# A new hand-off order for one kernel's 660 operations, with D loaded first, added as column plus scalar, and the first copy on one engine

## The chip, the cores and the metric

The kernel runs on one core of one Trainium2 chip. The core has TensorE (PE, matrix products), VectorE (DVE), ScalarE (ACT), GpSimd (POOL) and SyncE (SP, which here only issues DMAs). The metric is device time in microseconds, the median of several runs.

## The reference

Two blocks, each behind a layer norm without weights, on a sequence of S = 2048 rows of D = 640 columns in bf16:

```python
# block A: a short filter over k, times v, then a long convolution along S
k_shift = sum over t<4 of k_pad[:, t:t+S] * shift_k[:, 3-t]
kv = k_shift * v
y = irfft(rfft(kv, 2S) * rfft(ssm_k, 2S))[:, :S] + kv * ssm_D
h = x + layernorm(x) * y            # x is A_q
# block B: dense, mish, dense
z = layernorm(h) @ w1 + b1          # 640 -> 1728
h2 = h + (z * tanh(softplus(z))) @ w2
```

The input B_x is not used.

## The kernel before

**How the work is staged.** The convolution is done as two-step Fourier transforms by matrix products, with the 640 columns in five blocks of 128 ("dc" 0 to 4). For the convolution kernel ssm_k: a block is loaded (`d_n0` to `d_n4`), ssm_D is added to its first column (`dadd0` to `dadd4`, L364; so kv * ssm_D needs no pass of its own), PE transposes it (`k1pe`, L370), a copy takes it from PSUM to SBUF (`k1ev`, through the helper at L254 to L258: L256 when ScalarE does it, L258 when VectorE does), PE does the first step of the transform in four quarters (`s1kpe{dc}_{quarter}`, L390 and L391, 16 matrix products each) and each is copied out (`s1kev`). When all twenty are there, the second step follows in 22 pieces over 128 frequencies (`s2kpe_{f}`, L416; `s2kev`), and ten DMAs make a copy with the halves swapped (`sw{dc}_{half}`, L444). For k and v: k is loaded in four parts (`d_k`), transposed (`ktpe{m}_{part}`, L335, five ops of 4 x 4 transposes), copied out (`ktev`), its last rows shifted by one on GpSimd (`ktsh`, L339), filtered by matrix products with a band matrix (`kspe{m}_{half}`, L351 and L352; the four band matrices `wsh0` to `wsh3`, L311, are built from `coef`, L303), and multiplied by v as it leaves PSUM (`kv{m}_{half}`, L356). It then goes through the same two steps (`s1vpe`, `s1vev`, `s2v{chunk}pe`, `s2v{chunk}ev`; the chunks are the dc blocks 0, then 1 and 2, then 3 and 4). The spectra are multiplied on VectorE (`pr{dc}_{f}`, L455, 20 of 128 x 2048), and two inverse steps bring them back: `i1pe`/`i1ev` (L473, twenty quarters) and `i2` (L525, by row tile), with `y{t}` as the copy out.

Sixteen row tiles t then follow: statistics of x (`ln1_t`, L504 and L505), 1/sqrt on GpSimd (`ln1p`, L509 to L511), the normalised x (`lnx`, L516 on ScalarE or L518 on GpSimd), the product with y (`wb`, L532), the sum with x (`h`, L534), the second norm (`bn`, L538 to L540; `pow`, L542; `hc`, L544), and a transposition (`trpe`/`trev` by PE for tiles 0 and 1; `tr` by DMA, L557, for the others). The dense layers go by units of tiles: units 0 and 1 have two tiles each, units 2, 3 and 4 have four. `m1pe{unit}_{pair}` (L582, L589) is the first product, `hb` (L604) mish on ScalarE, `m2pe{t}` (L647, L655) the second product, which is finished for two tiles at a time, `res{t}` (L672, L669) adds h on VectorE, and `d_out{t}` (L676) stores.

**What sets the order.** `ORDER` (L26 to L61) lists all 660 operations in the sequence in which they are issued. Each engine runs its own operations in that sequence, and waits for data where it must. `@0` to `@3` names which of four PSUM tiles (two banks each) an operation of PE writes; the tile can be written again when its copy out is done. `:a`, `:d` and `:p` put an operation on ScalarE, VectorE or GpSimd where it has a choice; without a letter the first in its list is taken. Loads are issued from SP in the order of the list, except `d_cst`, `d_dr` (D itself, 5 KB) and `d_sk`, which are issued from ScalarE's queue. Besides data and tiles, a DMA's issue waits for one of eight semaphores that the DMAs of these two queues use in turn.

In a list of operations below "PE, then ..." gives a sequence on one engine.

Of the kernel before, what the change touches and what calls it, by code (L numbers as in the profile page):

```python
# [30 lines left out]
s1kev2_1 ktpe1_3 ktpe4_0@2 wsh3 d_g0 ktev1 ktpe4_2 ktpe0_0@1 ktpe4_1 ktpe4_3 ktpe2_0@0 ktev4 ktpe3_0@3 ktpe2_2 ktpe3_3 d_g4 ktpe3_2 ktpe3_1 ktpe2_1
ktev3 s1kpe1_1@2 ktpe2_3 s1kev1_1 ktpe0_3 ktev2 ktpe0_1 ktsh3 d_g5 ktpe0_2 s1kpe3_0@3 ktsh1 s1kpe2_0@2 ktev0 ktsh4 s1kev3_0 kspe4_1@0 d_g3 ktsh2
s1kev2_0 ktsh0 kspe3_0@3 kv4_1 s1kpe2_3@1 s1kpe4_2@2 kv3_0 s1kev2_3 s1kpe4_0@0 s1kev4_2 s1kpe2_2@1 s1kev4_0:d kspe4_0@3 s1kev2_2 kspe0_0@2 kv4_0
s2kpe_96@0 s2kpe_30@1 kv0_0 s2kev_96 kspe1_0@3 s2kev_30 s2kpe_42@0 kv1_0 s2kpe_24@2 s2kev_42 kspe2_0@1 s2kev_24:d s2kpe_120@3 s2kpe_108@0 s2kev_120
kv2_0 kspe1_1@2 s2kev_108 s2kpe_12@3 kv1_1 d_x0 s2kpe_36@1 s2kev_12 d_x1 kspe0_1@0 s2kev_36:d s2kpe_90@2 s2kpe_48@3 s2kev_90 kv0_1 kspe2_1@1 s2kev_48
s2kpe_78@2 kv2_1 s1vpe4_1@0 s2kev_78 s2kpe_6@3 s1vev4_1 s2kpe_66@1 ln1_1 s2kpe_84@2 s2kev_66 kspe3_1@0 s2kev_84:d ln1p1 s2kev_6 s2kpe_0@1 kv3_1
s2kpe_60@2 s2kev_0 s1vpe2_0@3 s2kev_60 d_x2 s1vpe2_2@0 s1vev2_0:d s1vpe2_1@1 d_x3 s1vev2_2 s1vpe0_1@2 lnx1:p s1vev2_1:d s2kpe_102@3 s1vev0_1
s2kpe_72@0 s2kev_102:d s1vpe1_0@1 s2kev_72 s1vpe3_0@2 s1vev1_0 s1vpe0_2@3 s1vev3_0:d s1vpe1_3@0 s1vev0_2 s2kpe_126@1 ln1_0 s2kpe_114@2 s2kev_126
s1vpe2_3@3 s1vev1_3 s2kev_114:d s2kpe_54@1 ln1p0 s1vev2_3 s2kpe_18@0 s2kev_54:d s1vpe0_0@2 s2kev_18 s1vpe4_0@3 ln1_3 s1vpe3_2@1 s1vev0_0 sw2_1
s1vpe4_2@0 sw1_0 s1vev3_2:d s1vev4_0 ln1p3 s1vpe1_2@2 sw1_1 s1vev1_2 sw3_1 s1vpe1_1@3 s1vev4_2:d lnx3:p s1vpe3_3@1 sw4_1 s1vev1_1 s1vpe0_3@2  # L40
s1vev3_3:d lnx0:p sw3_0 s1vpe4_3@0 s1vev0_3 sw0_0 s1vpe3_1@3 ln1_2 sw2_0 s2v1pe_112@1 s1vev4_3 s2v1pe_96@2 sw0_1 s1vev3_1:d s2v1ev_112 ln1p2 sw4_0
s2v1pe_48@0 d_t2m s2v1ev_48 s2v1ev_96:d s2v1pe_32@1 lnx2:p s2v1pe_64@3 s2v1ev_32 s2v2pe_80@0 pr1_96 b1pe@2 s2v1ev_64 s2v1pe_80@1 pr1_32 s2v2ev_80
s2v1pe_0@3 s2v1ev_80:d s2v1ev_0 s2v1pe_16@0 s2v1ev_16 s2v2pe_32@3 pr1_64 s2v2pe_0@1 c_b1 s2v2ev_32 s2v2pe_48@0 pr1_0 s2v2pe_64@2 s2v2ev_48 pr2_64
i1pe1_0@3 s2v2ev_0 s2v2pe_112@0 pr2_96 s2v2ev_64 i1pe1_1@1 i1ev1_0 pr4_32 s2v2pe_16@2 s2v2ev_112 i1pe1_2@3 pr2_0 s2v2ev_16 pr2_32 s2v2pe_96@0 i1ev1_1
s2v0pe_0@2 pr3_0 i1ev1_2 i1pe2_3@1 s2v0ev_0 pr3_32 s2v0pe_64@3 s2v2ev_96 i1pe2_0@2 pr3_64 s2v0ev_64 s2v0pe_96@0 pr3_96 i1ev2_3 s2v0pe_32@3 pr4_0
i1ev2_0 i1pe2_1@1 d_w10 d_w11 s2v0ev_96 i1pe3_1@2 pr4_64 d_w12 i1ev2_1 d_w14 i1pe3_2@0 pr0_0 d_w13 s2v0ev_32 i1pe3_3@1 pr4_96 i1ev3_2 i1pe3_0@3
i1ev3_3 pr0_32 i1pe4_2@0 i1ev3_0 i1pe4_1@1 pr0_96 i1ev3_1 i1pe1_3@3 ln1_6 i1ev4_2 i1pe4_3@2 pr0_64 ln1p6 i1ev1_3 i1pe2_2@0 i1ev4_1 ln1_5 i1pe0_0@3
lnx6:p i1ev2_2 i1pe0_2@1 ln1_9 ln1p5 i1ev0_0 i1pe0_1@0 ln1_4 lnx5:p i1ev0_2 i1pe0_3@3 i1ev0_1:d ln1p4 i1ev4_3 i1pe4_0@1 ln1_7 i1ev0_3 ln1p9 d_w2b
i1ev4_0 d_w2c ln1_11 i2a1@0 d_w2a ln1p7 i2a0@2 i2b0 ln1_14 i2b1 i2pe9@3 y0 i2pe4@1 y1 wb0 i2a3@2 y9 h0 i2pe11@0 wb1 y4 i2b3 h1 i2a2@3 y11 bn0 i2b2
i2pe10@1 y2 i2pe5@0 y10 bn1 i2pe7@3 pow0 y3 i2pe6@1 y7 i2pe12@2 wb3 pow1 y6 hc0 h3 trpe0@3 y12 i2pe13@1 hc1 trev0:a wb2 trpe1@2 bn3 trev1:a i2pe8@3  # L50
y13 m1pe0_4@2 h2 pow3 y8 bn2 lnx9 ln1p11 m1pe0_2@1 hc3 y5 m1pe0_6@3 wb6 tr3 pow2 hb0_2 wb5 m1pe0_1@0 w2z lnx7 hc2 ln1_10 tr2 m1pe0_3@1 hb0_4 lnx11:p
hb0_6 h5 m1pe0_0@2 ln1p14 lnx4 ln1_15 hb0_3 m1pe0_5@3 h6 hb0_0 bn6 m1pe1_5@1 hb0_1 wb7 lnx14 pow6 m1pe1_4@2 bn5 ln1p15 hb1_5 m1pe1_1@0 hb1_4 hc6 h7
tr6 pow5 hb0_5 m1pe1_2@1 bn7 ln1p10 hb1_1 m1pe1_0@2 hc5 ln1_12 pow7 tr5 m1pe1_6@3 hb1_0 hc7 ln1p12 hb1_2 ln1_8 tr7 m1pe1_3@0 hb1_6 wb11 i2pe14@2 h11
hb1_3 wb4 i2pe15@1 wb9 lnx10 m2pe0@3 h4 h9 y14 bn4 lnx12 ln1_13 pow4 ln1p8 hc4 m2pe2@0 wb10 tr4 h10 ln1p13 lnx8 bn11 lnx15 bn10 pow11 y15 lnx13 wb8
pow10 hc11 m1pe2_3@2 res2 wb12 d_out2 h12 tr11 h8 m1pe2_2@1 wb14 res0 bn8 d_out0 m2pe1@0 bn9 pow8 wb13 pow9 hc8 hc10 wb15 tr10 h13 h14 m1pe2_4@3 hb2_3
hc9 tr8 bn13 hb2_2 tr9 h15 pow13 m1pe2_5@2 bn12 bn14 pow12 m1pe2_6@1 hb2_5 hc13 bn15 tr13 hb2_4 m2pe3@2 hc12 pow15 hb2_6 tr12 pow14 hc15 hc14 tr14
tr15 m1pe3_1@3 res3 res1 d_out3 d_out1 m1pe3_6@1 hb3_1 m1pe3_0@2 hb3_6 m1pe3_2@0 hb3_0 m1pe3_4@3 hb3_2 m1pe2_1@1 hb3_4 m1pe3_5@2 hb2_1 m1pe2_0@0 hb3_5
m1pe3_3@3 hb2_0 m2pe4@1 hb3_3 m2pe6@2 m2pe5@0 res6 res4 d_out6 d_out4 m2pe7@3 m1pe4_3@2 res7 res5 d_out5 d_out7 m1pe4_5@1 hb4_3 m1pe4_2@3 hb4_5
# [108 lines left out]
def kernel(  # L167
# [193 lines left out]

    k1_pes, k1_evs = [], []
    for b in range(NDC):
        dad = OP(f"dadd{b}", ["dve", "pool"], [d_n[b], o_dc], emit=lambda e, b=b: (nc.gpsimd if e == "pool" else nc.vector).tensor_tensor(raw_n[b][:, 0:1], raw_n[b][:, 0:1], dcol[:, b:b + 1], ALU.add))  # L364
        p_ = pt()

        def pe(e, b=b, p_=p_):
            o = p_.b16().rearrange("p (t d) -> p t d", t=NT)
            for t2 in [*range(1, NT), 0]:
                nc.tensor.transpose(o[:, t2, :], raw_n[b][:, t2:S:16], ident)  # L370
# [347 lines left out]
```

## Time and profile before

| what | us |
|---|---|
| median of 3 runs (228.49 to 228.54) | 228.52 |
| the profiled execution | 227.92 |
| its span, first to last instruction | 226.13 |
| outside the span | 1.79 |
| first second-step copy of ssm_k (`s2kev_96`) starts on ScalarE | 32.86 |
| last copy of the first inverse step (`i1ev4_0`) starts on ScalarE | 92.46 |
| first matrix product of the dense layers (`m1pe0_4`) | 102.07 |
| last piece of the residual sum (`res15b`) starts | 223.16 |

The span has three parts. Up to about 33 us the inputs come in and PE, VectorE and ScalarE hand small pieces to each other. From there to about 102 us the convolution runs, in which VectorE and ScalarE have hardly a pause. From 102 us to the end PE has no pause in the dense layers. Times of single operations come from the timeline of each engine, matched to `ORDER` by counting instructions.

### The profile page before, as it was taken

Reading aid. Unit: us, or ns where it says so; the run is one execution under the profiler, and the core shown is the slowest. Engines: PE = TensorE matmul, PEld = TensorE weight load, DVE = VectorE, ACT = ScalarE, POOL = GpSimd, SP = SyncE. Lnnn points to the kernel's source line nnn. Section 1 sums busy time; section 2 is a strip of 40 time slices with the busy share of each in tenths; the row PEclk is TensorE's granted clock in tenths of the full one; section 3 lists DMA queues with packets and bytes.
Section 4 is the critical chain, followed back from the end, with each engine's and each line's share of the span. In section 5 each row is a group of like instructions: output and inputs, shape, how many; then the busy total and the mean of one; then the engine's idle time right before and its main releaser. Section 6 shows DMA issues by size and latency. Waiting matters only on the chain.

```text
...
## 1 busy us (share of the span) xinstructions
...
## 2 busy tenths in 40 slices
...
GB/s 206 371 421 415 418 343 33 210 232 97 414 412 206 167 259 4 185 192 33 29 77 38 62 58 89 137 12 3 0 0 58 29 32 0 3 29 46 58 53 48
DMA packets 19563, 30.98 MB, mean 137 GB/s; under 512 B 10704, under 2 KB 14928, under 8 KB 18768
## 3 DMA queue, kind: packets, MB, share of 16 engines
...
q8 instruction: 21, 0.34, 0.6%
...
q0 software_dynamic: 96, 0.00, 0.0%
HBM read 20.42 MB, written 2.62 MB: 102 GB/s over the span
## 4 chain that ended last, share of the span: by engine, by line
PE 67%; DMA 9%; DVE 9%; ACT 7%; SPq 3%; issue 3%; POOL 1%; DVEq 0%; ACTq 0%
PE ps L647 25%; PE ps L582 25%; DMA ks<-in_A_ssm_k_dram 6%; DVE ks L455 5%; PE ps L473 3%; ACT uv L256 3%; ACT ks L256 3%; SPq L444 3%; DMA ks<-ks 3%; PE ps L335 2%; PE ps L416 2%; PE ps L351 2%; PE ps L390 2%; PE ps L352 1%; PE ps L589 1%
## 5 line engine op out<-in xcount | busy, mean ns | idle before, releaser
L604 ACT ACTIVATE ks<-ps,b1s 128x512 bf16<-128x512 f32 (+1 forms) x69 | 36.2, 617 | 44.0 <-PE ps L582 35.8
L647 PE MATMUL ps<-ks 128*128 128x320 bf16 (+2 forms) x420 | 58.6, 299 | 0.0
L582 PE MATMUL ps<-G 128*128 128x512 bf16 (+1 forms) x325 | 57.6, 337 | 0.1
L672 DVE TENSOR_TENSOR rb<-ps,rb 128x640 bf16<-128x640 f32 x15 | 11.8, 820 | 68.4 <-PE ps L655 66.0
L647 PEld LDWEIGHTS <-ks 128*128 128x128 bf16 x420 | 40.6, 98 | 17.3 <-issue 1.3
L582 PEld LDWEIGHTS <-G 128*128 128x128 bf16 x325 | 31.3, 98 | 24.7 <-issue 1.6
L256 ACT CAST uv<-ps 128x1024 bf16<-128x1024 f32 x50 | 46.6, 1145 | 0.0
L256 ACT CAST ks<-ps 128x640 bf16<-128x640 f32 (+3 forms) x46 | 37.9, 898 | 10.1 <-PE ps L391 6.7
L455 DVE TENSOR_TENSOR ks<-ks,uv 128x2048 bf16<-128x2048 bf16 x20 | 23.0, 1221 | 0.8 <-DMA ks<-ks 0.6
L416 PEld LDWEIGHTS <-G 128*128 128x128 bf16 x512 | 20.9, 96 | 3.1 <-issue 2.5
L473 PE MATMUL ps<-a_t,ks 128*128 128x128 bf16 x320 | 19.2, 219 | 1.3 <-DVE ks L455 1.2
L473 PEld LDWEIGHTS <-ks 128*128 128x128 bf16 x320 | 18.2, 113 | 1.8 <-DVE ks L455 1.6
L509 POOL TENSOR_SCALAR ve<-mv 128x1 f32<-128x1 f32 x16 | 4.7, 294 | 48.2 <-DVE mv L505 47.3
L542 POOL TENSOR_TENSOR r<-ve,mhalf 128x1 f32<-128x1 f32 x16 | 10.2, 638 | 21.7 <-DVE ve L540 21.7
L416 PE MATMUL ps<-uv,G 128*128 128x64 bf16 (+1 forms) x384 | 12.9, 187 | 1.7 <-ACT uv L256 1.4
L538 DVE BATCH_NORM_STATS2 st<-rb 128x6 f32<-128x320 bf16 x32 | 14.1, 482 | 0.1
L258 DVE CAST ks<-ps 128x1024 bf16<-128x1024 f32 (+1 forms) x12 | 14.0, 1179 | 0.2
L504 DVE BATCH_NORM_STATS2 st<-rb 128x6 f32<-128x320 bf16 x32 | 13.9, 475 | 0.0
L356 DVE TENSOR_TENSOR ra<-ps,rb 128x1024 bf16<-128x1024 f32 x10 | 11.9, 1219 | 1.1 <-PE ps L352 0.7
L258 DVE CAST uv<-ps 128x1024 bf16<-128x1024 f32 x10 | 11.9, 1211 | 0.5 <-PE ps L391 0.2
L390 PE MATMUL ps<-cst,ks 128*64 128x128 bf16 x160 | 10.8, 220 | 0.9 <-DVE ks L258 0.5
L390 PE MATMUL ps<-cst,ra 128*64 128x128 bf16 x160 | 10.5, 219 | 0.8 <-ACT uv L256 0.5
...
## 6 DMA issues: line engine op xcount, KB each, us to landing
...
```

What stands on the lines that cost most here:

```text
L256: nc.scalar.copy(o, i)
L258: nc.vector.tensor_copy(o, i)
L356: nc.vector.tensor_tensor(kv_w[:, m, :, 8 * h:8 * h + 8, :], p_.f32().rearrange("p (l t d) -> p d t l", l=4, t=8), raw_v[:, 8 * h:8 * h + ...
L390: nc.tensor.matmul(ps[0:64, dgl, :], lhs, mc, start=True, stop=True)
L416: nc.tensor.matmul(p_.f32()[:, o:o + n], g_v[:, f, :], src[:, :, f, :], start=True, stop=True)
L455: nc.vector.tensor_tensor(o, o, v, ALU.mult)
L473: nc.tensor.matmul(pz[:, dgl, :], KS[:, k, b, :, l], a12[:, k, :], start=k == 0, stop=k == 1)
L504: nc.vector.bn_stats(st1[:, t, hh, :], xt(t)[:, hh * 320:(hh + 1) * 320])
L538: nc.vector.bn_stats(st2[:, t, hh, :], xt(t)[:, hh * 320:(hh + 1) * 320])
L582: nc.tensor.matmul(ph[:, o:o + w], w1[:, dc, fc * P:fc * P + P], lt[:, dc, 0:w], start=dc == 0, stop=dc == NDC - 1)
L604: nc.scalar.activation(hb[:, fc, 0:n], p_.f32()[:, i * 512:i * 512 + n], ACT.Mish, bias=b1s[:, fc:fc + 1], scale=1.0)
L647: nc.tensor.matmul(p_.f32()[:, o:o + n], lhs, w2[:, k, cols:cols + n], start=fc == 0, stop=single and fc == 13)
```

## The change

The chunks and all sizes stay. Three small edits:

```diff
-dad = OP(f"dadd{b}", ..., (gpsimd or vector).tensor_tensor(raw_n[b][:, 0:1], raw_n[b][:, 0:1], dcol[:, b:b + 1], ALU.add))
+dad = OP(f"dadd{b}", ..., (gpsimd or vector).tensor_scalar(raw_n[b][:, 0:1], raw_n[b][:, 0:1], dcol[:, b:b + 1], None, ALU.add))
...
-k1_evs[b].append(OP(f"k1ev{b}" + "b" * h, ["act", "dve"] if h else ["dve", "act"], ...
+k1_evs[b].append(OP(f"k1ev{b}" + "b" * h, ["dve"] if b in K1S else ["dve", "act"], ...
```

The first makes the addition of D a column plus a per-partition scalar. The second takes away the choice for the two half copies of block 0: both are VectorE's (`k1ev0` was ScalarE's). The third is a new `ORDER`, all of it. Its beginning, and the stretches that are spoken of later:

```diff
-d_cst wz idn d_n0 cz d_dr wm@0 small lane d_n1 d_sk d_n3 warm d_n4 d_k2 kz d_a12 dsel dcol d_k0 dadd0:p k1pe0@1 d_n2 dadd1 d_k3 k1pe1@2 k1ev0b:d
-k1ev0:a d_k1 s1kpe0_3@3 k1ev1 s1kpe0_0@0 s1kev0_3 dadd3:p d_v2 s1kpe0_2@1 s1kev0_0:d s1kpe0_1@2 k1pe3@3 s1kev0_1 dadd4:p d_v3 s1kev0_2:d cfpe@0
...
+d_dr wz idn d_n0 cz wm@0 small lane d_n1 d_cst d_sk d_n3 warm d_n4 d_a12 kz d_n2 dsel dcol dadd0 k1pe0@1 d_k1 dadd1:p d_k3 k1pe1@2 d_k0 k1ev0b d_v3
+k1ev0 s1kpe0_2@3 k1ev1 s1kpe0_1@0 s1kev0_2 d_k2 s1kpe0_0@1 dadd3 s1kev0_0 s1kpe1_0@2 s1kev0_1:d d_v2 s1kpe1_3@3 s1kev1_0 d_v0 cfpe@1 k1pe3@0 coef
...
+s1kev3_3 ktsh0 s1kev2_2:d s1kpe1_2@0 s1kpe1_1@2 s1kev1_2 kv2_0 s1kpe2_3@3 s1kev1_1 s1kpe2_0@0 s1kev2_3:d kspe2_1@1 s1kev2_0 kspe3_0@2 kv2_1
+s2kpe_102@3 s2kpe_120@0 kv3_0 s2kev_102 kspe4_0@1 s2kev_120 s2kpe_18@3 kv4_0 s2kpe_114@2 s2kev_18 kspe0_0@0 s2kev_114 s2kpe_108@1 kv0_0 kspe1_0@3
...
```

What moves, engine by engine:

- **SP's queue** before: n0 n1 n3 n4 k2 a12 k0 n2 k3 k1 v2 v3 g1 v0 v1 and seven more g; after: n0 n1 n3 n4 a12 n2 k1 k3 k0 v3 k2 v2 v0 g3 g6 v1 and six more g. `d_x3` goes behind the ten `sw`, `d_t2m` behind four of the five `d_w1`. The two queues of DMAs together are the same set.
- **Copies**: `ktev0` and `ktev3` (128 x 2048) go from VectorE to ScalarE, `s2v1ev_80` and `s2v1ev_96` too; some thirty others change engine, so that ScalarE has 17 of the 22 `s2kev` instead of 16 and 12 of the 20 `s1vev` instead of 13.
- **GpSimd**: `wsh2` goes to VectorE; `dadd1`, `dadd2` and `dadd4` are GpSimd's (they were `dadd0`, `dadd3` and `dadd4`); `lnx` of tiles 4, 7, 8, 9, 10, 12 and 15 goes from ScalarE to GpSimd, which then has 14 of the 16. Tiles 8, 5 and 4 are normalised among the products `pr3`, and 10, 9, 12 and 15 follow in a row behind `pow6` and `pow4` (`pow6 pow4 lnx10 lnx9 lnx12 pow7 lnx15 pow11 pow5`).
- **The dense layers** before: units 0 and 1, `i2pe14`, `i2pe15`, then `m2pe0 m2pe2 m1pe2_3 m1pe2_2 m2pe1 m1pe2_4 ...`; after: units 0 and 1, the same two, then `m2pe1@2 m2pe3@1 m2pe0@3 m1pe2_3@0 m1pe2_0@1 m1pe2_6@0 m2pe2@2 m1pe3_0@1 m1pe3_1@2 m1pe2_5@3 ...`. VectorE's list beside it: `... wb5 hc6 h8 h11 hc4 bn7 h5 bn11 bn5 wb10 hc7 hc11 wb13 wb9 hc5 wb12 wb15 wb14 bn8 h13 res3 h14 h10 hc8 h15 h9 bn9 bn10 bn13 hc10 hc9 res1 bn14 bn15 hc13 h12 hc14 bn12 res2 ...`.
- **The end** before: `m2pe11 m2pe13 res11 res9 m2pe15b res13 res15b`; after: `m2pe12 m2pe14 m2pe15b res12 res14 res15b`, with the stores `d_out12 d_out14 d_out15b` last.

More of the change, by code (lines that the diff above doesn't have):

```diff
@@ L31 @@
[L31 to L58, printed above, removed]
@@ new lines @@
+s1kev1_3 dadd2:p d_g3 dadd4:p k1pe2@2 wsh3 k1ev3:a k1pe4@1 d_g6 k1ev2 s1kpe0_3@3 k1ev4 wsh1 s1kpe3_2@0 d_v1 s1kev0_3 s1kpe3_0@2 s1kpe4_3@1 s1kev3_2
+s1kev3_0:d s1kpe2_1@3 d_g7 s1kev4_3 wsh0 s1kpe4_0@0 s1kev2_1:d s1kpe3_1@2 s1kev4_0 ktpe3_0@1 d_g1 ktpe3_3 s1kev3_1:d s1kpe4_2@3 ktpe0_0@0 s1kev4_2
+ktpe3_1 wsh2:d ktpe1_0@2 d_g2 ktpe3_2 ktpe0_1 ktev3:a ktpe1_2 ktpe0_2 ktpe1_3 ktpe1_1 ktpe2_0@3 ktev1 ktpe2_2 d_g4 ktpe0_3 ktpe4_0@1 ktev0:a ktpe2_3
+ktsh1 ktpe4_3 ktpe2_1 d_g0 ktsh3 s1kpe4_1@2 ktev2 ktpe4_1 ktpe4_2 s1kev4_1 kspe1_1@0 ktev4 ktsh2 s1kpe2_2@3 d_g5 kv1_1 s1kpe3_3@2 ktsh4 kspe2_0@1
@@ new lines @@
+s1vpe3_0@2 s1vev3_3 sw3_1 s2v1pe_112@1 lnx3:p sw0_0 ln1_0 s1vev3_0 s1vpe0_3@3 sw4_0 s2v1pe_16@0 s2v1ev_112 pr2_64 sw3_0 ln1p0 s2v1pe_48@2 d_x3
+s2v1ev_16 s2v1pe_32@1 s1vev0_3:d lnx0:p s2v1ev_32 s1vpe3_1@0 pr1_64 s1vpe0_0@3 s2v1ev_48 s2v1pe_0@1 s1vev0_0:d s1vev3_1 s2v1ev_0 pr2_32 s2v2pe_32@2
+s2v2pe_112@0 s2v2ev_32 s1vpe0_1@3 pr2_0 s2v2ev_112 s2v2pe_48@1 s2v2pe_64@2 pr1_32 s1vev0_1 s2v2pe_0@0 pr2_96 s2v2ev_64 s2v0pe_32@3 s2v2ev_0
+s2v2pe_80@2 pr1_0 s2v2ev_48 i1pe2_0@0 pr1_96 s2v0ev_32 s2v2pe_16@1 ln1_8 s2v2ev_80 s2v0pe_0@3 pr3_32 s2v2ev_16 ln1p8 i1pe1_0@2 s2v0ev_0 ln1_5 lnx8:p
@@ new lines @@
+i1pe1_3@1 i1ev1_0 pr3_64 ln1p5 s2v2pe_96@3 i1ev2_0 s2v0pe_96@2 ln1_4 lnx5:p s2v2ev_96 s2v0pe_64@0 pr3_0 s2v0ev_96 ln1p4 i1pe1_2@3 d_w13 i1ev1_3 d_w12
+pr3_96 i1pe2_1@2 lnx4:p d_w14 i1ev1_2 d_w11 i1pe2_2@1 pr0_32 d_t2m s2v0ev_64 d_w10 i1pe2_3@3 pr0_0 i1ev2_1 i1pe3_3@0 i1ev2_2 pr0_96 i1pe3_0@2 i1ev2_3
+i1pe3_2@1 pr0_64 i1ev3_0 i1pe3_1@3 pr4_96 i1ev3_2 i1pe1_1@2 pr4_32 i1ev3_3 i1pe0_2@1 i1ev1_1 pr4_0 i1pe0_0@0 i1ev0_2 i1pe0_3@2 pr4_64 i1ev0_0
+i1pe0_1@1 ln1_7 i1ev3_1 i1pe4_3@0 ln1_6 i1ev0_3 ln1p7 i1pe4_2@3 i1ev4_3 ln1_11 i1pe4_1@2 ln1p6 i1ev0_1 i1pe4_0@0 i1ev4_2:d lnx7:p i1ev4_1 i2a0@1 d_w2b
@@ new lines @@
+ln1_13 i2a1@3 lnx6:p i1ev4_0 d_w2c b1pe@2 d_w2a ln1_15 ln1p11 c_b1 i2b0 i2a3@0 y0 i2b1 i2a2@2 y1 wb0 i2b3 i2pe13@1 h0 y3 i2pe12@3 wb1 y13 bn0 i2b2
+i2pe10@0 y2 i2pe11@1 y12 h1 i2pe4@2 pow0 y11 bn1 i2pe7@3 y4 i2pe8@1 y7 wb3 i2pe6@2 pow1 hc0 y8 h3 trpe0@3 y6 i2pe9@1 hc1 wb2 trev0:a trpe1@2 h2
+lnx11:p trev1:a i2pe5@3 bn2 y9 w2z m1pe0_5@2 y10 bn3 pow2 y5 m1pe0_2@1 hb0_5 hc2 pow3 wb4 m1pe0_6@0 tr2 hb0_2 ln1p13 m1pe0_4@3 hc3 wb6 tr3 wb8
+m1pe0_1@2 ln1p15 hb0_4 ln1_9 hb0_6 m1pe0_0@1 hb0_1 h6 ln1p9 ln1_12 lnx13 m1pe0_3@3 hb0_0 wb7 ln1p12 m1pe1_0@0 ln1_10 hb0_3 m1pe1_4@2 h7 hb1_0 ln1p10
```

22 lines of the change are left out of this document (16 added, 6 removed).

## The prediction

> **What bounds the kernel now.** I read the busy time of each engine in stretches first, cut where the timelines of ScalarE and PE change character.
>
> ```profile
> core 0: us, PE busy (x) PEld busy (x) DVE busy (x) ACT busy (x) POOL busy (x), PEclk, DMA share, GB/s
> 0.00:32.86 32.86, 29.89 (x564) 25.12 (x565) 24.45 (x31) 18.03 (x19) 14.47 (x28) 1.00 0.95 371
> 32.86:93.37 60.51, 56.08 (x1245) 52.51 (x1243) 58.47 (x72) 59.28 (x67) 13.49 (x28) 1.00 0.55 194
> 93.37:102.07 8.70, 8.24 (x65) 4.72 (x63) 8.39 (x25) 8.28 (x15) 3.80 (x8) 1.00 0.65 233
> 102.07:223.10 121.03, 121.03 (x821) 75.14 (x820) 48.93 (x124) 45.85 (x83) 20.62 (x38) 1.00 0.16 40
> 223.10:226.13 3.03, 0.03 (x1) 0.00 (x0) 0.42 (x1) 0.00 (x0) 0.00 (x0) 1.00 0.22 76
> ```
>
> From 102.07 PE is busy in every microsecond, at full clock: 121.03 us of dense products that the change does not touch. So a gain can only come from starting them earlier, and a loss also from holes in them. From 32.86 to 93.37 ScalarE and VectorE are both full (59.28 and 58.47 of 60.51 us). Before that neither is. The timelines of the first 17 us show where the hand-offs stall:
>
> ```profile
> 6.82 0.16 DVE L364 TENSOR_TENSOR ks<-ks,dcol 128x1 bf16<-128x1 bf16 x1 [0.80 <-DMA ks<-in_A_ssm_k_dram]
> 6.89 0.68 DVE L258 COPY ks<-ps 128x1024 bf16<-128x1024 bf16 x1
> 7.61 1.01 ACT L256 COPY ks<-ps 128x1024 bf16<-128x1024 bf16 x1 [3.63 <-DVE ks L258]
> ...
> 12.71 8.14 POOL L311 TENSOR_TENSOR rw<-cst,coef 128x1120 bf16<-128x1120 bf16 x4 [2.77 <-DVE coef L303]
> 15.30 1.52 DVE L364 TENSOR_TENSOR ks<-ks,dcol 128x1 bf16<-128x1 bf16 x1
> 16.87 0.28 PE L370 MATMUL ps<-ident,ks 128*128 128x128 bf16 x1 [0.41 <-DVE ks L364]
> ```
>
> The two halves of block 0's copy ran one behind the other although on two engines, the first behind `dadd1`. `dadd2`, one column, took 1.52 us instead of 0.16: it ended at 16.82, when GpSimd's second `wsh` did (16.80), and PE's last transposition of block 2 waited for it.
>
> **The first 33 us.** I laid out the new order by hand. An operation starts when its engine is free, its input is there and its PSUM tile was copied out, with start-to-start times from the timelines: a block of 16 transpositions 1.15 us, an `s1kpe` 0.45, a `ktpe` 0.25, a `kspe` 0.83; a copy of 1024 takes 0.91 on ScalarE (1.01 until its data can be used) and 1.13 on VectorE (1.22), one of 2048 1.86 and 1.13.
> - *D first.* D landed at 5.54, issued at 1.11; issued at 0.72 it lands 0.4 earlier. That is worth nothing: `dadd0` ended at 6.29, and PE's last transposition of block 0 began at 6.40, at its own pace.
> - *The addition.* On GpSimd a column of such a form costs 0.22 to 0.29 (L509) for 0.19: nothing, since PE reads that column last, 1 us behind the first. `dadd2` now stands ahead of the `wsh`: 1.4 us of VectorE and 0.4 of PE go.
> - *Both halves on VectorE.* 6.69 to 7.36 and 7.30 to 7.98 (0.68 each), for 7.58 and 8.62. PE is with block 1 until 7.92, so `s1kpe0` starts no earlier, but its second half at 8.37, not 8.68, and ScalarE is spared 1.01.
> - *Block 2's load* goes ahead of two 640 KB parts of k, 1.55 us each by the landings: 15.28 becomes about 12.2. All that is then late is k part 2, at 19.9 for 18.3 or so, and one `ktpe` waits some 0.4 us.
> - *The end of this stage* goes: `ktev0` on ScalarE ends 24.2, `kspe1_1` 25.2, `kv1_1` on VectorE 25.8 to 27.0 (behind `ktev4`), `s1kpe1_2` in its tile 27.7, `s1kev1_2` 27.75 to 28.75, `s1kpe2_0` 29.45, `s1kev2_0` 29.55 to 30.55, PE in `kspe3_0` until 31.0, `s2kpe_102` to 31.6, and its copy starts at 31.6.
>
> A layout by hand has no small gaps; I take **31.8** for 32.86. Ends: 31.1 if k's part 2 and block 2 land in time, 32.5 if each of some ten hand-offs loses 0.1 more.
>
> **From there to the last copy of the inverse step (ScalarE).** Before: start 32.86, last copy ends its share at 93.37: 60.5 us, of which 58.5 by counts (15 `s2kev` at 0.855 and a short one 0.31, 13 `s1vev`, 18 `s2v` copies and 19 `i1ev` at 0.905 to 0.91) and 2.0 are gaps (0.71, 0.70 and five small ones). After: one `s2kev` more, one `s1vev` fewer, two `s2v` copies more: +0.86 - 0.91 + 1.82 = +1.8, so 60.3. In the layout the two gaps of 0.7 shrink to 0.5 together, the small ones stay: 1.2 in all. 31.8 + 60.3 + 1.2 = **93.3**. What ScalarE was given is thus as much as the early start brings. VectorE loses two `s2v` copies and an `s2kev`, gains an `s1vev` and a statistic: -2 x 1.15 - 1.07 + 1.15 + 1.03 = -1.2, and would be free for `wb0` at about 92.3, where y0 ends at 94.0: no bound, with 1.5 us in hand. The swaps are issued about 52.6 (54.23 before) and the first two land 4.9 later, 57.5, just as VectorE comes to `pr2_64` (57.7). `d_t2m` behind four weight loads: issued about 80, landed by 89 at the 8.7 us of its row, wanted at 92. `wsh2` on VectorE, not shown before: between 0.65 (half of L455's 2048) and 2.06 us (its row on GpSimd); I take 1.3, the middle; VectorE waits there for k's part 2 anyway, from 19.1 to 21.6, so even 2.06 is hidden.
>
> **To the first dense product.** The same chain of y0, y1, `wb`, `h`, `bn`, `pow`, `hc`, `trpe`, `trev`: 8.70 us, so 102.0 for 102.07.
>
> **The dense layers.** PE's 121.03 us stay if it never waits. The narrow place is new: `m2pe2` wants tile 2 of PSUM, which `res1` frees. On PE: 16.2 us (units 0 and 1, two `i2pe`), three `m2pe` (10.97), two `m1pe2` at 2.215 and one at 1.78: 33.4 us after the first product. On VectorE: its list down to `res1` by start-to-start times (`wb` and `h` 0.40, `hc` 0.36, statistics 1.04, `bn` 1.22, `res` 0.73) ends 31.9 after the first product, if GpSimd never holds it up. Before, `res2` was ready 2.7 us before `m2pe1` wanted it. GpSimd does hold it up:
>
> ```profile
> 105.72 1.38 POOL L489 MEMSET ks<- 64x640 bf16 x2
> 107.10 0.86 POOL L518 TENSOR_SCALAR ra<-rb,r,nmr 128x640 bf16<-128x640 bf16 x1
> ```
>
> ```profile
> 105.70 0.83 DVE L544 TENSOR_SCALAR rw<-rb,mv,r 128x640 bf16<-128x640 bf16 x1 [0.44 <-POOL r L542]
> 107.48 0.82 DVE L534 TENSOR_TENSOR rb<-ks,rb 128x640 bf16<-128x640 bf16 x1
> 109.25 0.44 DVE L534 TENSOR_TENSOR rb<-ks,rb 128x640 bf16<-128x640 bf16 x1
> ```
>
> A sum that takes 0.44 took 0.82 and ended 0.34 after GpSimd's normalisation did; that is 0.4 us a time, and 0.8 in that stretch with one normalisation and the clearing. Now five normalisations are there: 0.8 + 4 x 0.35 = 2.2 if each hits such an operation, 0.8 if none does. About half do: 1.5, so `res1` ends at 33.4, when PE wants it. I take **0.3** us of holes (0 to 0.7).
>
> The Trainium skill, "SBUF — State Buffer", section "Who interferes with whom", says that a VectorE instruction with two SBUF inputs and a GpSimd instruction that reads SBUF exclude each other for the whole instruction. The trace agrees: `dadd2` ended with the `wsh`, the sum at 107.48 went on when the normalisation had ended. By that rule alone each of the four added normalisations may cost up to its 0.87: 0.8 + 3.5 - 1.5 = 2.8 us of holes, and about 231.3.
>
> **The end.** `res12` and `res14` (0.73 apart) fit under `m2pe15b`'s 1.5 us, but `d_out14` is issued just ahead of `d_out15b`, and of two stores in a row the second landed 0.5 later (181.92 behind 181.42): +0.1, at most 0.5.
>
> **The sum.** Span 226.13 - 0.07 (start) + 0.3 + 0.1 = 226.46, +0.33 on the profiled execution of 227.92. That run lies 0.60 under the median of the runs; on the median it is 228.52 + 0.33, **228.8 us**. A change under 0.2% (0.46 us) is about what a measurement of this kernel cannot tell from none.
>
> **The rivals.**
> - *The lead is kept (faster).* ScalarE starts at 31.3, its gaps are 0.6, PE has no hole: 31.3 + 60.3 + 0.6 = 92.2, -1.2, end +0.1: 227.4 (226.9 to 228.0). For it: 1.4 us of stall at `dadd2` really goes. Against: ScalarE is full, and gets 1.8 more.
> - *GpSimd holds VectorE (slower).* Past 1.5 us of hold-up between `hc1` and `res1`, each further one is a hole on PE in front of `m2pe2`, and 8, 5 and 4 among the products cost VectorE its 1.5 us before `wb0` likewise. With 2.2 to 2.5 in each: holes 0.7 to 1, first product 0.5 later: 229.9 (229.0 to 231.3). Against: VectorE's statistics, half its time there, were not held up in the rows.
> - *The early lead is not there (slower).* ScalarE starts at 32.2 with gaps of 1.6, so that its 1.8 more are not paid: 94.1, +0.7, holes and end +0.4: 229.6 (229.0 to 230.4). For it: the layout has nothing spare in it.
> - *The small edits do nothing by themselves:* D's early landing is idle here, as worked out; inside the forecast.
>
> **Chances.** Forecast, within 0.2%: 0.32, with a range of its own of 228.1 to 229.0. Kept lead 0.28. GpSimd 0.22, no lead 0.18: slower 0.40. Range for 8 in 10, cutting a tenth off the outermost cases on each side: 227.1 to 230.7.
>
> **What would show it.** `dadd2` on GpSimd at 0.2 to 0.3 us and no wait of PE for it; the first `s2k` copy on ScalarE at 31.1 to 32.5; ScalarE without gaps from there to about 93.3; `wb0` waiting for y0, not for VectorE; first dense product near 102.0; PE busy 121.0 us from there, or a hole before `m2pe2` with VectorE's `res1` as releaser; VectorE's `wb`, `h` and `hc` at 0.8 beside GpSimd's `lnx`. I am wrong if the first `s2k` copy is off by over 0.7 us, or if ScalarE waits in the product stage for `pr` results.

## The result and the profile after

The changed kernel is a little faster, by 0.2 to 0.4% in three comparisons, of which the last does not exclude no change. In the first comparison it takes 227.65 us (median of 19 runs, 227.05 to 228.72) where the kernel before takes 228.53 (19 runs), a ratio of 0.9959 [0.9945, 0.9973]. Run again unchanged on other chips it stood at 0.9982 [0.9966, 0.9997] and 0.9984 [0.9964, 1.0003], while the kernel before, run against itself, gave 1.0002 [0.9989, 1.0016] and 1.0002 [0.9982, 1.0022]. The forecast was no change, 228.8 us.

A trap stands at the start: the two profiled executions say the opposite of the medians. The changed kernel's took 228.13 us and the kernel before's 227.92. What the profiled times hang on is shown below; why the medians differ is not shown in full. The stretches of the changed kernel, cut at the same events as those shown of before (first copy `s2kev` on ScalarE, end of the last inverse copy's share, first dense product, last residual piece):

```profile
core 0: us, PE busy (x) PEld busy (x) DVE busy (x) ACT busy (x) POOL busy (x), PEclk, DMA share, GB/s
0.00:32.71 32.71, 30.20 (x564) 25.50 (x565) 22.65 (x31) 20.30 (x20) 12.77 (x27) 1.00 0.94 366
32.71:93.69 60.98, 56.97 (x1246) 53.41 (x1244) 57.88 (x73) 60.91 (x68) 27.80 (x36) 1.00 0.60 213
93.69:102.29 8.60, 7.96 (x63) 4.70 (x63) 8.26 (x24) 8.26 (x16) 3.90 (x7) 1.00 0.29 106
102.29:223.34 121.05, 120.73 (x815) 75.21 (x820) 47.56 (x122) 40.76 (x76) 22.06 (x39) 1.00 0.14 39
223.34:226.36 3.02, 0.01 (x1) 0.00 (x0) 0.42 (x1) 0.00 (x0) 0.00 (x0) 1.00 0.37 130
```

The first stretch is 0.15 us shorter, the second 0.47 longer, the third 0.10 shorter, the dense layers the same to 0.02. (Their row shows 0.32 us less of PE and six products fewer. The stretch is no longer for it, and the same kernel's second profile has all 821 products in the same time, so I take these for records that the trace lost.) ScalarE's idle time in the second stretch went from 1.23 us (60.51 less 59.28) to 0.07: it has more copies and no pauses. The timelines show where the pauses were. Before, and then after:

```profile
32.86 2.68 ACT L256 CAST ks<-ps 128x960 bf16<-128x960 f32 x3 [1.03 <-DVE ra L356]
36.13 2.68 ACT L256 CAST ks<-ps 128x960 bf16<-128x960 f32 x3 [0.59 <-PE ps L416]
39.40 2.68 ACT L256 CAST ks<-ps 128x960 bf16<-128x960 f32 x3 [0.59 <-PE ps L416]
```

```profile
32.71 8.02 ACT L256 CAST ks<-ps 128x960 bf16<-128x960 f32 x9 [1.03 <-DVE ra L356]
```

Nine copies stand in one row with no wait ahead of the later ones. And the two small stalls of the first stage are gone. GpSimd's two additions in the changed kernel, ahead of its `wsh`, and the two halves of block 0's copy on VectorE:

```profile
11.77 0.53 POOL L364 TENSOR_SCALAR ks<-ks,dcol 128x1 bf16<-128x1 bf16 x2 [3.88 <-DMA ks<-in_A_ssm_k_dram]
12.63 6.11 POOL L311 TENSOR_TENSOR rw<-cst,coef 128x1120 bf16<-128x1120 bf16 x3 [0.33 <-PE ps L370]
```

```profile
6.89 1.29 DVE L258 COPY ks<-ps 128x1024 bf16<-128x1024 bf16 x2 [1.39 <-PE ps L370]
```

In their place PE waits for a DMA, on the line that transposes k (L335). PE's waits in the first 33 us of the changed kernel (total, times, longest):

```profile
PE ps L286 <- DVE rw L281: 1.2, 1, 1.2
PE ps L370 <- DMA ks<-in_A_ssm_k_dram: 0.6, 1, 0.6
PE ps L335 <- DMA ra<-in_A_k_dram: 0.3, 1, 0.3
```

The 0.6 us on L370 (0.2 before) is the wait for block 1. The last row, 0.3 us, is the one that sets the time of the changed kernel's profiles, as the third group of experiments shows.

### The profile page after: what moved, and what is told of

Same layout as the page of the kernel before. It is cut to its first block, busy times and chain, and to the rows that moved or that the text cites. A ratio compares the mean times of both kernels' runs of the same rounds, so it can differ in the third digit from the quotient of the medians.

```text
span 226.4 us, 6193 instructions
## 1 busy us (share of the span) xinstructions
PE 215.9 (95%) x2684; PEld 158.8 (70%) x2690; DVE 136.8 (60%) x248; ACT 130.2 (58%) x177; POOL 66.5 (29%) x107
## 4 chain that ended last, share of the span: by engine, by line
PE 63%; DVE 16%; DMA 11%; ACT 6%; SPq 2%; issue 1%; ACTq 0%; DVEq 0%
PE ps L647 25%; PE ps L582 25%; DVE ks L455 10%; DMA ra<-in_A_k_dram 5%; ACT ks L256 3%; DMA ks<-in_A_ssm_k_dram 3%; DMA ks<-ks 2%; ACT uv L256 2%; PE ps L335 2%; DVE st L504 2%; PE ps L351 2%; SPq L444 1%; PE ps L416 1%; PE ps L473 1%; PE ps L390 1%
## 5 line engine op out<-in xcount | busy, mean ns | idle before, releaser
L256 ACT CAST uv<-ps 128x1024 bf16<-128x1024 f32 x51 | 47.3, 1173 | 0.0
L256 ACT CAST ks<-ps 128x960 bf16<-128x960 f32 (+3 forms) x47 | 38.1, 907 | 9.4 <-PE ps L391 8.1
L455 DVE TENSOR_TENSOR ks<-ks,uv 128x2048 bf16<-128x2048 bf16 x20 | 23.6, 1239 | 1.4 <-DMA ks<-ks 1.4
L518 POOL TENSOR_SCALAR ra<-rb,r,nmr 128x640 bf16<-128x640 bf16 x14 | 15.9, 1141 | 2.7 <-DVE ks L532 1.3
L509 POOL TENSOR_SCALAR ve<-mv 128x1 f32<-128x1 f32 x16 | 6.2, 388 | 35.3 <-DVE mv L505 34.4
L542 POOL TENSOR_TENSOR r<-ve,mhalf 128x1 f32<-128x1 f32 x16 | 10.1, 636 | 17.3 <-DVE ve L540 17.2
L416 PE MATMUL ps<-uv,G 128*128 128x64 bf16 (+1 forms) x384 | 13.4, 187 | 1.8 <-ACT uv L256 1.8
L510 POOL TENSOR_TENSOR r<-ve,mhalf 128x1 f32<-128x1 f32 x16 | 13.1, 819 | 1.3
L258 DVE CAST ks<-ps 128x1024 bf16<-128x1024 f32 (+1 forms) x11 | 12.9, 1187 | 0.4 <-PE ps L416 0.3
```

Source lines behind the costliest of these rows:

```text
L256: nc.scalar.copy(o, i)
L416: nc.tensor.matmul(p_.f32()[:, o:o + n], g_v[:, f, :], src[:, :, f, :], start=True, stop=True)
L455: nc.vector.tensor_tensor(o, o, v, ALU.mult)
L510: nc.gpsimd.tensor_tensor(r1[:, t:t + 1], ve1[:, t:t + 1], mhalf[:], ALU.pow)
L518: nc.gpsimd.tensor_scalar(lnx_s[t % 9], xt(t), r1[:, t:t + 1], nmr1[:, t:t + 1], ALU.mult, ALU.add)
```

## The experiments

Times are medians; each ratio is to the kernel before on the same chip. "Base B" is the kernel before, "base A" the changed one. Two distances recur: from PE's start on block 1 (`k1pe1`, which as a rule starts 0.05 us behind the landing of block 1) to ScalarE's first `s2kev`, and from there to the first dense product. The "front" is the part up to that `s2kev`, the "back" what follows.

**Which half holds the gain.** The changed order up to its first `s2kpe`, then the old one, and the reverse; the filter pieces that one half had already done were exchanged for those that it had not.

```diff
 fa_bb: ... kspe3_0@2 kv2_1          (changed order)
+       s2kpe_96 ...                 (order before, to the end)
 fb_ba: the order before up to s2kpe_96
+       s2kpe_102 s2kpe_120 ...      (changed order, to the end)
```

> The changed kernel once more, for a second profile. Theory F (the gain is made in the first 33 us, and the first profile caught a late execution): ratio to before 0.994 to 0.998, and a profile whose first second-step copy of ssm_k starts earlier than the 32.71 us of the first profile, at 31.5 to 32.3, with the first dense product at 101 to 102. Theory B (the gain is made after 33 us): the same ratio, but first copy again at 32.5 to 33 and the way from it to the first dense product 0.5 to 1 us shorter than the 69.2 us of before.

> The kernel before once more, against itself: ratio 0.998 to 1.002. Its profile is to show how far two executions of one kernel lie apart. Theory F: first second-step copy at 32.9 or later (the first profile, 32.86, was an early one, its execution 0.6 us under the median). Theory B: 32.7 to 33, and the way from there to the first dense product longer than 69.2 us.

> The changed kernel's first 33 us (its list up to kv2_1, with the two small edits), then the list of before from its first second-step piece on, with kspe and kv renamed so that each block half is still filtered once. Theory F: 0.5 to 1.5 us faster than before (0.993 to 0.998). Theory B: within 0.3 us of before, or slower.

> The first 33 us of before, then the changed kernel's list from its first second-step piece on, renamed likewise. Theory F: no gain, 0 to 1.5 us slower than before, since ScalarE has 1.8 us more copies and no earlier start to pay them from. Theory B: 0.5 to 1 us faster than before.

Unchanged kernels: 0.9982 and 1.0002; a_again's first `s2kev`, 31.98 us, is what theory F expected, b_again's, 32.40, is not. Hybrids: 229.42 (1.0056 [1.0043, 1.0068]) and 229.68 (1.0069 [1.0056, 1.0082]), both slower than either parent, by 1.3 us and more. Theory F fails in the first hybrid, theory B in the second. That an order fits the state in which the stretch before leaves engines and tiles, and loses at a joint, is argued, not shown. In fa_bb the dense layers take 121.88 us, not 121.09. In fb_ba ScalarE's first `s2kev` is 0.75 us further behind block 1 than in base B; why was not traced. Such hybrids tell little of the halves.

**The addition alone, and the order without the small edits.**

```diff
 b_ts (on base B)
-tensor_tensor(raw_n[b][:, 0:1], raw_n[b][:, 0:1], dcol[:, b:b + 1], ALU.add)
+tensor_scalar(raw_n[b][:, 0:1], raw_n[b][:, 0:1], dcol[:, b:b + 1], None, ALU.add)
 a_noedits (on base A)
-tensor_scalar(...) ; d_dr first, d_cst later ; k1ev0 on VectorE
+tensor_tensor(...) ; d_cst first, d_dr later ; k1ev0 on ScalarE
```

> The kernel before with one edit: the addition of D as column plus scalar, order unchanged, so dadd2 still stands beside GpSimd's wsh. Theory P (the one-column tensor_tensor was held by GpSimd's wsh, which a form with one SBUF tensor is not): dadd2 0.15 to 0.3 us for 1.25 to 1.7, the first second-step copy 1.0 to 1.4 us earlier than 32.4 to 32.9; but the products wait for the swapped copies afterwards, so the kernel is only 0.2 to 0.7 us faster. Rival (the column waits for something else, such as the landing of block 2): dadd2 unchanged and the time within 0.3 us of before.

> The changed kernel's order without the small edits: tensor_tensor for the addition, the table of cosines ahead of D on ScalarE's queue, the first half copy back on ScalarE. Theory O (the order makes the gain, the small edits are idle): within 0.3 us of the changed kernel, 0.995 to 0.999 of before. Rival (the small edits make it): 0.5 us or more slower than the changed kernel, 0.999 to 1.003; of the three, the half copy would show as the second s1kpe0 piece starting 0.3 to 0.6 us later.

b_ts: 227.08, **0.9948 [0.9936, 0.9960]**: one word of base B does at least as much as the whole change, two of whose three intervals lie above this one. VectorE in b_ts, then GpSimd in b_ts:

```profile
15.07 0.21 DVE L364 TENSOR_SCALAR ks<-ks,dcol 128x1 bf16<-128x1 bf16 x1
```

```profile
12.66 8.14 POOL L311 TENSOR_TENSOR rw<-cst,coef 128x1120 bf16<-128x1120 bf16 x4 [2.77 <-DVE coef L303]
```

The column is added in 0.21 us in the midst of GpSimd's products; as two tensors it took 1.52, 1.25 and 1.66 in three profiles of base B and ended with the second product each time. The Trainium skill, "SBUF — State Buffer", "Who interferes with whom", states that a VectorE instruction with at most one SBUF input, outside the two-port modes, does not contend with GpSimd; the 0.21 agrees. From block 1's start to the first `s2kev` base B needs 26.09, 26.07 and 26.11 us, b_ts 24.79 (the five kernels built on it 24.78 to 25.27): the 1.3 us reach the end of the stage whole. Behind it b_ts has 69.21 us, base B 69.21, 69.52 and 69.22, so the loss that was expected there did not come. a_noedits: 227.32, 0.9965 [0.9952, 0.9977]: in the new order `dadd2` stands ahead of GpSimd's `wsh` and takes 0.19 us as two tensors as well. The ratio of the order alone lies among the changed kernel's three, as theory O expected. The stall can be removed by form or by place; done twice it is not worth twice.

**What ends the front in the changed kernel.**

```diff
 a_k2 (on base A):       ... k1ev0b
+d_k2 d_v3 ...
-d_v3 ... s1kev0_2 d_k2 ...
 a_cst (on base A):
-d_dr ... d_n1 d_cst ...
+d_cst ... d_n1 d_dr ...
 a_cst_k2: both
 b_ts_dr (on b_ts):
-d_cst ... cz d_dr ...
+d_dr ... cz d_cst ...
 b_ts_k1 (on b_ts): both halves of block 0's copy on VectorE
 b_ts_n2 (on b_ts): d_n2 moved ahead of d_k2 and d_k0
```

> The changed kernel with k's part 2 loaded ahead of v's part 3 (one place earlier in SP's queue). Theory K (the front of the changed kernel ends with the landing of k's part 2, at 20.0 to 20.7): part 2 lands 1.5 us earlier, PE does not wait in ktpe3_2, first second-step copy 0.3 to 0.5 us earlier, the kernel 0.2 to 0.5 us faster than the changed one (0.994 to 0.997 of before). Rival (the hand-offs of PSUM tiles bind there, not the load): no change, 0.996 to 0.998.

> The changed kernel with the cosine table's transfer issued ahead of D's again. Theory (D first puts the table's 104 KB in the way of block 1's load, by the 0.4 us by which that load lands later in every profile with D first): block 1's load lands at 6.3 to 6.8, ScalarE's first copy of a scaled tile starts at 31.5 to 31.9, and the time is 0.3 to 0.5 us below the changed kernel's, a ratio of 0.994 to 0.996 to the kernel before. Rival (D first costs nothing, the landings differ by chance): the changed kernel's time, 0.996 to 0.998.

> The same kernel, and k's part 2 is loaded ahead of v's part 3. Theory (two costs of the new front, block 1's load late by 0.4 us and part 2 of k late by some 0.2 us): both gains add, 0.992 to 0.995 of the kernel before. Rival (only one of the two ends the front at a time): the ratio of the better one alone, 0.995 to 0.996.

> The kernel before with the addition as column plus scalar, and D's transfer issued ahead of the cosine table's. Theory (D first delays block 1's load): 0.3 to 0.5 us slower than with the addition's form alone, a ratio of 0.996 to 0.997 to the kernel before, block 1's load landing at 6.9 to 7.5. Rival (D first costs nothing): 0.995, as with the form alone.

> The kernel before with the addition as column plus scalar, and both half copies of block 0 on VectorE. Theory (ScalarE is free for block 1's copy sooner, and the constant between block 1's landing and ScalarE's first scaled copy shrinks by some 0.3 us): a ratio of 0.993 to 0.994 to the kernel before. Rival (the copy waits for block 1's landing whichever engine takes the half): 0.995, as with the form alone.

> The kernel before with the addition as column plus scalar, and block 2 of ssm_k loaded ahead of k's parts 2 and 0. Theory (block 2's late landing at 14.9 still ends the front, through PE's transpositions of it at 15.2): ScalarE's first scaled copy 0.3 to 1.0 us earlier, 0.991 to 0.993 of the kernel before. Rival (PE has other work ahead of block 2, or a later part of k takes its place as the last input): no gain, 0.994 to 0.997.

> The changed kernel, unchanged, a third time. Theory (its front is 0.8 to 1.0 shorter from block 1's start, block 1 starts 0.5 later, its back is 0.3 longer): a distance of 25.0 to 25.3 from block 1's start to ScalarE's first scaled copy, first dense product 69.5 to 69.7 behind that, a ratio of 0.996 to 0.998. Rival (the first measurement was the chance one, the kernels are equal): 0.999 to 1.001.

> The kernel before, unchanged, a third time. Theory (the stall of the second block's addition varies with where it meets GpSimd's product, and that is what spreads this kernel's times): the addition takes 1.2 to 2.0 us in the profile, and ScalarE's first scaled copy starts 25.9 to 26.6 behind PE's start on block 1. Rival (the landings alone vary): the distance is 26.1 as in the two profiles before, only block 1's start moves. Ratio 0.999 to 1.001.

| kernel | block 1 lands | k part 2 lands | first `s2kev` | profiled time |
|---|---|---|---|---|
| after | 7.41 | 20.67 | 32.71 | 228.13 |
| a_again | 6.83 | 19.96 | 31.98 | 227.49 |
| a_again2 | 6.68 | 21.22 | 33.24 | 228.66 |
| a_noedits | 6.53 | 20.30 | 32.33 | 227.75 |
| a_cst | 6.56 | 20.11 | 32.13 | 227.58 |
| a_k2 | 6.99 | 18.74 | 31.95 | 227.69 |
| a_cst_k2 | 6.62 | 18.05 | 31.35 | 226.77 |

In the first five the first `s2kev` starts 12.02 to 12.04 us behind the landing of k's part 2, whatever block 1 did, and the whole time is that landing plus 207.44 to 207.53; a_ln8, of the next group, adds a sixth (12.04 and 207.47). So this load, and little else that varies, sets the time of these executions. In the first three PE waits 0.35, 0.20 and 0.87 us for it. a_again2 was expected 25.0 to 25.3 us behind block 1 and came out at 26.51: my theory that block 1 sets this front fell with it. PE's row at that place in a_again2, and in a_cst_k2, where the load goes ahead of v's part 3:

```profile
21.27 0.90 PE L335 MATMUL ps<-ident,ra 128*128 128x128 bf16 x11 [0.87 <-DMA ra<-in_A_k_dram]
```

```profile
18.81 3.40 PE L335 MATMUL ps<-ident,ra 128*128 128x128 bf16 x50
```

With the load ahead the wait is gone, PE comes to part 2 some 1.1 to 1.4 us behind its landing, and the distance from block 1 is 24.9 and 24.7: now block 1 sets the front. a_k2: 227.29, 0.9959 [0.9946, 0.9971], which is theory K's; a_ln8, whose front is the changed kernel's own, stood at 227.98 on the same chip. a_cst: 227.54, 0.9965 [0.9945, 0.9986]; its theory fell, since block 1 landed early, at 6.56, and the first `s2kev` stayed 12.02 us behind part 2, at 32.13. Neither interval is clear of the changed kernel's. **Both: 226.91, 0.9949 [0.9930, 0.9969]**, 0.63 us below a_cst on the same chip.

D first is not free. Where it is first, block 1 lands at 6.68 to 7.41 (seven profiles, mean 7.05); with the cosine table first at 6.24 to 7.43 (thirteen, mean 6.63). The lists overlap, the means differ by 0.42. GB/s over the first 6 us in steps of 0.15, in base B and in the changed kernel:

```profile
GB/s 0 0 0 0 0 0 0 0 0 0 0 50 94 288 348 285 109 0 27 218 218 328 382 437 410 358 333 278 341 415 328 382 437 411 383 367 308 291 204 167
```

```profile
GB/s 0 0 0 0 0 0 0 0 0 0 0 0 0 0 6 18 256 137 109 137 191 273 191 355 328 382 393 329 335 358 380 395 416 416 421 382 410 410 345 372
```

With the table first, the six steps from 1.65 us on move some 175 KB, the table's 104 KB and the beginning of block 0. With D first (5 KB) they move some 40 KB: three of them are empty, and the table moves later, among the blocks. An estimate: the table's 104 KB at the 300 GB/s or so of these rows are 0.35 us. The Trainium skill, "DMA: Bandwidth & Descriptors", "Issuing engines are not separate DMA queues", says that DMAs of all issuing engines run on the same 16 DMA engines and interleave; these rows agree. What it costs in time is less firm: b_ts_dr 227.58, 0.9985 [0.9959, 1.0011], against b_ts's 0.9948 [0.9936, 0.9960], intervals that just touch, block 1 at 7.18. A cost of the size that was expected is thus possible and not shown.

Two edits are worth nothing that can be measured on top of b_ts. b_ts_k1: 226.92, 0.9947 [0.9928, 0.9966], distance 24.90; its theory fell, the rival holds. b_ts_n2: 226.70, 0.9946 [0.9927, 0.9965]; block 2 lands at 10.82, not 14.90, and the distance is 24.82. In b_ts PE is at other work until it comes to block 2 at 15.2, as the rival had it.

b_again2 (1.0002) ends another idea, that the stall's length spreads base B's times: the stall was 1.66 us and the distance still 26.11.

**What ends the stretch to the dense layers.**

```diff
 a_ln8 (on base A): ln1_8 moved ahead of pr1_64, into VectorE's wait for a swap
 b_ts_act (on b_ts):
-s2v1ev_96:d ... s2v1ev_80:d
+s2v1ev_96:a ... s2v1ev_80:a
 ck_i1 (on a_cst_k2):
-i1ev4_1 ... ln1_13 ... ln1_15 ... hc1
+i1ev4_1:d ... hc1 ln1_13 ln1_15
```

> The changed kernel with the statistics of tile 8 put ahead of pr1_64 on VectorE, where it waits 1.2 us for the fourth swapped copy. Theory V (the products on VectorE end the convolution in the changed kernel): the last product 0.8 to 1.0 us earlier relative to the first second-step copy, ScalarE's wait of 0.4 to 0.5 us before i1ev4_3 gone, the first dense product 0.3 to 0.5 us earlier, 0.994 to 0.997 of before. Rival (ScalarE's copies end it, as I predicted): the products earlier, the first dense product within 0.2 us of the changed kernel's place, 0.996 to 0.998.

> The kernel before with the addition as column plus scalar, and two copies of the second step of v (frequencies 80 and 96 of chunk 1) on ScalarE, not VectorE. Theory (ScalarE alone ends the stretch to the first dense product, every copy given to it costs its 0.91 us, less the gap of 0.7 that it closes): 1.1 to 1.8 us slower than with the form alone, a ratio of 1.000 to 1.003 to the kernel before, ScalarE without gaps. Rival (waits for products and swaps set its gaps, so the added copies fill idle time and make VectorE's products earlier): within 0.3 us of the form alone, 0.994 to 0.996.

> The changed kernel with the cosine table ahead of D and k's part 2 ahead of v's part 3 (0.9949 before), and one more inverse copy (quarter 1 of block 4) on VectorE, the statistics of tiles 13 and 15 behind the first two sums. Theory (ScalarE alone ends the stretch, VectorE has 0.7 us in hand there): first dense product 0.4 to 0.9 us earlier, 0.991 to 0.993. Rival (PE's inverse step or VectorE is as late as ScalarE): no gain, 0.994 to 0.996, or a loss if the two statistics come too late for a row tile.

a_ln8: 227.98, 0.9993 [0.9979, 1.0007]. VectorE's last product ended 0.5 us earlier (88.33 for 88.87) and the first dense product did not move (69.58 us behind the first `s2kev` in both): VectorE does not end this stretch. Its ratio is worse than the rival's 0.996 to 0.998, and nothing in its profile explains that. b_ts_act: 228.69, **1.0031 [1.0013, 1.0049]**, and the distance to the first dense product is 71.05 for 69.21: the two copies cost 1.84 us, which is their own length twice, 0.91 each; the theory holds. VectorE, spared them, only waited, and for ScalarE (waits of VectorE between 57 and 70 us, b_ts and then b_ts_act):

```profile
DVE ks L455 <- DMA ks<-ks: 0.4, 2, 0.2
```

```profile
DVE ks L455 <- ACT uv L256: 3.8, 3, 1.9
```

ck_i1 takes a copy from ScalarE and gains 0.33 of its 0.91 us: the first dense product stands 69.25 behind the first `s2kev`, 69.58 in a_cst_k2. That is no more than base B's own 69.21 to 69.52, so the gain itself is not firm, and the theory's 0.4 to 0.9 did not come. From there more than that is lost: 228.74, 1.0018 [0.9997, 1.0040]. The inverse products on PE, ScalarE behind them, and PE's one hole in the dense layers, all of ck_i1:

```profile
84.82 6.37 PE L473 MATMUL ps<-a_t,ks 128*128 128x128 bf16 x109
```

```profile
91.22 1.01 ACT L256 CAST uv<-ps 128x1024 bf16<-128x1024 f32 x1 [0.23 <-PE ps L473]
```

```profile
109.98 6.17 PE L582 MATMUL ps<-G 128*128 128x256 bf16 x55 [1.80 <-ACT ks L604]
```

PE runs without a pause up to `i2a0` at 91.05, and ScalarE's last copy now waits for it: as a bound PE is only some 0.3 us behind ScalarE. The hole of 1.80 us came with the two later statistics, behind which VectorE's `wb2` now stands; the path between them was not tried apart.

**GpSimd's normalisations alone.**

```diff
 b_ts_lnx (on b_ts)
-lnx4 lnx7 lnx8 lnx9 lnx10 lnx12 lnx15
+lnx4:p lnx7:p lnx8:p lnx9:p lnx10:p lnx12:p lnx15:p
```

> The kernel before with the addition as column plus scalar, and the seven normalisations that the change gives to GpSimd (tiles 4, 7, 8, 9, 10, 12, 15) on GpSimd in their old places. The prediction's rival (GpSimd holds VectorE's sums, half of them or more): 0.8 to 2.8 us of holes on PE or of a later first dense product, a ratio of 0.998 to 1.007, VectorE's products, wb and h longer than in the kernel with the form alone. Theory now (VectorE's instructions run back to back and GpSimd is the one that is held, as the long lnx in the changed kernel suggest): no hole in PE's 121.0 us, 0.994 to 0.996, GpSimd's lnx above 1 us in the mean.

227.77, 0.9982 [0.9967, 0.9997]: some 0.8 us slower than b_ts. The prediction's rival has the right size, at its low end, and my later theory of no cost fell. Up to the first dense product the two are equal (69.22 and 69.21 us); the loss is in the dense layers, 122.07 us for 121.32. Holes on PE (both in b_ts_lnx):

```profile
108.24 6.28 PE L582 MATMUL ps<-G 128*128 128x256 bf16 x55 [0.20 <-DMA G<-rw]
125.36 4.48 PE L582 MATMUL ps<-G 128*128 128x512 bf16 x19 [0.44 <-DMA G<-rw]
```

PE waits for a row tile's transposition by DMA, which waits for `hc` on VectorE. VectorE's and GpSimd's groups of the dense layers, b_ts_lnx first and then the changed kernel (busy, mean ns, idle before them and its releaser):

```profile
L532 DVE TENSOR_TENSOR ks<-ks,ra 128x640 bf16<-128x640 bf16 x16 | 8.3, 526 | 0.0
L534 DVE TENSOR_TENSOR rb<-ks,rb 128x640 bf16<-128x640 bf16 x16 | 8.1, 520 | 0.2
L544 DVE TENSOR_SCALAR rw<-rb,mv,r 128x640 bf16<-128x640 bf16 x16 | 7.3, 463 | 2.6 <-POOL r L542 2.6
```

```profile
L532 DVE TENSOR_TENSOR ks<-ks,ra 128x640 bf16<-128x640 bf16 x16 | 7.4, 482 | 0.0
L534 DVE TENSOR_TENSOR rb<-ks,rb 128x640 bf16<-128x640 bf16 x16 | 7.7, 496 | 0.1
L544 DVE TENSOR_SCALAR rw<-rb,mv,r 128x640 bf16<-128x640 bf16 x16 | 7.3, 472 | 0.1
```

```profile
L518 POOL TENSOR_SCALAR ra<-rb,r,nmr 128x640 bf16<-128x640 bf16 x14 | 15.9, 1141 | 2.7 <-DVE ks L532 1.3
```

In b_ts_lnx VectorE waits 2.6 us for `pow` (1.0 in base B), because `pow` stands in GpSimd's own queue among the normalisations, and its products `wb` (L532) and sums are longer (base B: 480 and 505 ns). Most of those waits come too late to matter: 1.2 us of them lie behind the second hole. What delays that hole's transposition, issued 1.48 us later behind the first dense product than in b_ts, is 0.48 us of `pow` and some 1.0 us by which two `wb` and a sum were held beside GpSimd's normalisations. The longest case is beside two normalisations in a row. Two `wb` on VectorE from 118.02 on take 1.40 us together, 0.89 in b_ts, and GpSimd's row there is:

```profile
117.60 3.22 POOL L518 TENSOR_SCALAR ra<-rb,r,nmr 128x640 bf16<-128x640 bf16 x2
```

So here the prediction's hold-up is seen, on both engines at once. In the changed kernel VectorE waits 0.1 us for `pow`, its `wb` and sums are no longer than base B's (482 and 496 ns), and it is GpSimd's normalisation that is stretched, to 1141 ns from 870.

## Why the prediction was wrong

The median moved by -0.4 to -0.9 us where +0.33 was forecast. The mechanism of the gain was seen (b_ts has 1.3 us of it); the terms set against it failed. ScalarE's gaps were put at 1.2 us, and 0.5 of that was not there; the holes in the dense layers (0.3) and the later end (0.1) were not there at all. With the start as forecast and everything behind it as measured the sum would have been -0.68 us.

- **End of the first stage, 31.8 for 32.86: the layout holds, the landing under it was too early.** Three profiles give 31.98, 32.71 and 33.24, base B's 32.86, 32.40 and 32.77, so in the means the profiles show no lead. By its own sign (off by over 0.7 us) the prediction is wrong here in two of the three; that k's part 2 was the risk, it had said. The layout had k part 2 at 19.9; by the 12.03 us that the profiles show behind that landing this is 31.9. It lands at 19.96 to 21.22. The profiled execution of the changed kernel had 20.67; its median, 227.65, would answer to 20.2 (less 207.46), a first `s2kev` at 32.2; no trace shows that execution.
- **D first, worth nothing: wrong.** Only D's own consumer was followed. D landed at 2.89 us for 5.54, not 0.4 earlier, and the table at 5.48 for 2.71: the two changed places. The table that it displaced, and block 1 behind that, land later, by 0.42 us in the means.
- **The addition, 1.4 us: right** (1.3 in b_ts, and it goes in the changed order either way). **Both halves on VectorE and block 2's load**: idle by themselves (b_ts_k1, b_ts_n2). They were given no price of their own, but the layout leaned on them.
- **ScalarE's stretch, +1.0 (61.5 for 60.5): mis-sized.** It measured +0.47, 60.98, of which 60.3 are the copies as counted and 0.7 gaps. Its copies do cost their length (b_ts_act). The step that failed first is "the two gaps of 0.7 shrink to 0.5 together, the small ones stay: 1.2 in all": neither of the large ones was left.
- **To the first dense product**: 8.60 for 8.70, as forecast. First `s2kev` to first dense product in all: 69.58, 69.67 and 69.59 for 69.21, 69.52 and 69.22, +0.3.
- **Holes of 0.3 before `m2pe2`: wrong.** PE has none, 121.09 us to the last residual piece in both. VectorE's sums were not lengthened; "about half do" was taken from one row of 0.82 us. By the Trainium skill's rule ("SBUF — State Buffer", "Who interferes with whom") read the same way, with VectorE the loser, it would have been 231.3; the section also says that the order of issue decides who blocks, and here GpSimd was mostly the one held.
- **The end, +0.1: not there** (3.02 and 3.03 us).
- **The offset of 0.60 from profile to median: wrong as a step.** It was carried over from base B. For the changed kernel it is -0.48, and +0.18 and -0.89 in the other two profiles, since k's landing varies by 1.26 us between them. Between the two profiled executions the sum was near, +0.33 for +0.21, but by luck, two errors that cancel: a start 0.9 later than laid out (32.71 for 31.8), and all that stands behind it 1.0 shorter (193.65 us of span for 194.66).

On the medians: the back costs 0.3, so the front must have brought 0.7 to 1.2. That is inferred, not shown, and the profiles' means do not bear it out. All three profiles of base B (227.92, 227.75, 227.85) lie 0.3 to 0.6 below its medians, so no trace shows its median run; what is longer there stays open. For the addition alone both agree: b_ts lies 1.15 us under base B's mean in the profiles, 0.98 in the medians. Of the rivals, "the lead is kept" (227.4) came nearest, with no gap on ScalarE and no hole on PE, though with a later start; the hold-up by GpSimd is real in another order (b_ts_lnx) and did not come in this one.

Two simpler or corrected versions came out lowest: base B with the addition's form alone (0.9948), and the changed order with two loads put back (0.9949). Between them nothing can be told apart, and both intervals overlap that of the changed kernel's first comparison.
